# A two-network attention kernel: zero products while the first keys load, first loads reordered over two queues, first K^T copied from PSUM, key tails and weight conversions re-timed

## The chip, the cores and the metric

The kernel runs on one core of a Trainium2 chip. The metric is the device time of one execution in microseconds (us). The kernel before took 880.57 us (median of three runs, 880.42 to 881.54).

A core has five engines that run their own instruction streams and meet at semaphores: TensorE (PE, with its weight loads shown as PEld), VectorE (DVE), ScalarE (ACT), GpSimd (POOL) and SyncE (SP). SP and ACT issue the transfers here; 16 DMA engines carry them out.

## The reference

Three stages follow each other: windowed attention, a feed-forward network with g(h) = h·cos(h), and one with g(h) = relu(h)². Shapes: 4 batches, 8 heads, 512 local and 32 global positions, head size 64; the networks take 2176 tokens of 512 features through 2048 hidden ones.

```python
k_all, v_all = concat([k_g, k_l]), concat([v_g, v_l])
out_g = softmax(scale * q_g @ k_all.T) @ v_all
s_ll = where(|pos_i - pos_j| <= 32, scale * q_l @ k_l.T, -1e9)
out_l = softmax(concat([scale * q_l @ k_g.T, s_ll])) @ concat([v_g, v_l])
x = concat([out_g, out_l]) in token order       # 2176 x 512
h = x @ moe_w_in;  x = (h * cos(h)) @ moe_w_out
h = maximum(x @ moe2_w_in, 0);  out = (h * h) @ moe2_w_out
```

## The kernel before, in words

**Attention.** Heads are worked in pairs p = 0 to 15 (`divmod(p, 4)` gives batch and pair). Four heads of one batch, two pairs, are a group; there are eight. A group's keys and queries arrive in natural layout (`kn`, `qn`, two buffers each), are transposed on PE (`tr_k` L295, `tr_q` L338), and leave PSUM as `kT` and `qT`. `kT` holds, for each of eight blocks of 64 positions, three pieces: the block (`k_evac`, ACT, L306), the next block (`k_copy`, POOL, L321) and the 32 global keys (POOL, L323). The piece after the last block is the "tail" of K: its own small load (`load_ktn`, L367), a transpose (`ttail`, L350) and a copy into `kT` by POOL (L331). The values come in twice: `va` from DRAM (`load_v`, L270 and L273) and `vb`, the same rows moved by 64 partitions, by a copy inside the chip (`copy_v`, L280 and L281) that needs `va` complete. `vgz` (L286) has the global values.

**Steps.** The list of items is per group Local, Local, Local, Local, Global: 40 in all. A loop over steps s issues, for each step, parts of several items at fixed distances (`CFG["lag"]`) and in a fixed order (`CFG["order"]`): item s gets its scores S (L388, for a Global L514) and its softmax, item s-2 its transposes (`tw`, L456), item s-3 their copies out of PSUM (ACT, L462 and L466), item s-4 its output products (`o`, L472 with `vgz`, L484 with `va`, then with `vb`; a Global's `og`, L590). Since each engine runs its instructions in this order, one that waits holds up all behind it.

**Loads.** SP has nearly all loads in one queue, in the order of the program; ACT issues only the first group's queries. Before the loop stand the loads of group 0 (in two halves of two heads), its tail and values, and the keys of group 1; in the loop's first steps `vgz`, the queries of group 1 and the copies `vb` follow.

**Weights of the first network.** They arrive as pairs of 32-bit words and are converted during attention in six pieces: `conv_load` (L117, L122), `conv_u` (POOL, L142), `conv_s` (ACT, L147), then DVE and POOL steps. `piece` asks for the load at step 5 + 3i and for the first conversions two steps after it; `put` finds for each the first step from there that has room on its engine. `thalves` splits tokens for the first network and asks for their store to DRAM (`x_store`, L720) in the step after the last part is made.

**Networks.** From about 160 us on PE is the full engine (L823 and L915), and a planner lays out the instructions. The last block has 640 tokens in five tiles of 128; each tile's sum is made by DVE (L926) and stored by SP at once (L1004). The tile with the global rows is stored in four pieces (L1008).

Of the kernel before, what the change touches and what calls it, by code (L numbers as in the profile page):

```python
# [11 lines left out]
F32 = mybir.dt.float32  # L12
# [3 lines left out]
AF = mybir.ActivationFunctionType  # L16
# [4 lines left out]
P = 128  # L21
# [31 lines left out]
def kernel(  # L53
# [14 lines left out]
    nc = tc.nc  # L68
    B, H, SL, D = q_l.shape
    SG = q_g.shape[2]  # L70
# [167 lines left out]
    kn, qn, kT, qT, tks = {}, {}, {}, {}, {}  # L238


    def load_k(gi, sub=4):
        b, h0 = gi // 2, 4 * (gi % 2)
        t = fp.tile([P, 4, 4, D], F32, tag="kn", name="kn", bufs=2)
        kn[gi] = t
        for i in range(0, 4, sub):
            d, g = slice(i, i + sub), slice(h0 + i, h0 + i + sub)
            nc.sync.dma_start(t[0:SG, 0, d], k_g[b, g].rearrange("h p d -> p h d"))
            for c in range(4):
                r0 = SG if c == 0 else 0
                nc.sync.dma_start(  # L250
                    t[r0:P, c, d],
                    k_l[b, g, P * c - SG + r0 : P * c + P - SG].rearrange("h p d -> p h d"),
                )

    def load_q(gi, queue=nc.sync, heads=((0, 4),)):
        b, h0 = gi // 2, 4 * (gi % 2)
        if gi not in qn:
            qn[gi] = fp.tile([P, 4, 4, D], F32, tag="qn", name="qn", bufs=2)
        u = qn[gi]
        for i, sub in heads:  # L260
            d, g = slice(i, i + sub), slice(h0 + i, h0 + i + sub)
            for c in range(4):
                queue.dma_start(
                    u[:, c, d], q_l[b, g, P * c : P * c + P].rearrange("h p d -> p h d")
                )

    def load_v(gi):
        b, h0 = gi // 2, 4 * (gi % 2)
# [22 lines left out]
    def tr_k(p):  # L291
# [9 lines left out]
        kT[p] = t  # L301
        tks[p] = tk

    def k_evac(p):
        t, tk = kT[p], tks.pop(p)
        nc.scalar.activation(  # L306
            t[:, :, 0:64], tk.rearrange("p (j q) -> p j q", q=64), AF.Copy
        )
        if CFG["kb"] == "A":
            nc.scalar.activation(  # L310
                t[:, :, 128:KTB], tk[:, 0:SG].unsqueeze(1).to_broadcast([P, 8, SG]), AF.Copy
            )
        elif CFG["kb"] == "D":
            nc.vector.tensor_copy(
                t[:, :, 128:KTB], tk[:, 0:SG].unsqueeze(1).to_broadcast([P, 8, SG])
            )

    def k_copy(p):
        t = kT[p]
        one = dict(scalar1=1.0, scalar2=1.0, op0=ALU.mult, op1=ALU.mult)  # L320
        nc.gpsimd.tensor_scalar(t[:, 0:7, 64:128], t[:, 1:8, 0:64], **one)  # L321
        if CFG["kb"] == "P":
            nc.gpsimd.tensor_scalar(  # L323
                t[:, :, 128:KTB], t[:, 0, 0:SG].unsqueeze(1).to_broadcast([P, 8, SG]), **one
            )
        if p > 1:
            k_tail(p)
# [275 lines left out]
            )  # L603


    load_q(0, nc.scalar, ((0, 2),))
    load_k(0, 2)
    nc.vector.memset(halfpi, 0.5 * math.pi)
    nc.scalar.activation(warm, halfpi, AF.Exp)
    load_q(0, nc.scalar, ((2, 2),))  # L610
    load_ktn(0)
    load_qgn(0)
    load_v(0)
    load_k(1)
    make_identity(nc, ident)
    nc.gpsimd.memset(masks[0], 0.0)
    for h in range(2):
        s = slice(64 * h, 64 * h + 64)
# [9 lines left out]
        nc.vector.tensor_copy(masks[i], masks[0])  # L628
    nc.vector.memset(masks[1][0:64, 0:32], NEG)
    nc.vector.memset(masks[2][64:128, 96:128], NEG)  # L630
    nc.vector.memset(qgbd, 0.0)

    nc.gpsimd.memset(ktail, 0.0)
    nc.gpsimd.memset(VGZ[0], 0.0)
    nc.vector.memset(VGZ[1], 0.0)
    for t in VA:
        nc.vector.memset(t[32:64, 4], 0.0)

    items = []
    due_tr, due_load = {}, {}  # L640
# [155 lines left out]
    class Step:  # L796
# [99 lines left out]
        def jobs(self):  # L896

            if self.net == 0:
                return [(e, t) for t in (1, 0) for e in range(NK)]
            tiles = range(2 * self.n // P)  # L900
            late = [j for j in tiles if j * P >= self.n]
            return [(j, 1) for j in late] + [(j, 0) for j in tiles if j not in late]

        def job(self, j, t, k):
            n = self.n
# [11 lines left out]
        def y_out(self, j, t, eng):  # L917
            n, c0 = self.n, self.c0
            y = self.r.pop(("y", j, t))
            if self.net == 0:  # L920
                y, dst = y[:, 0:n], xt[:, j, c0 + t * n : c0 + t * n + n]
            else:
                y = y.rearrange("p (k t) -> p k t", k=NK)
                dst = xt[:, :, c0 + j * P : c0 + j * P + P]
            if not self.first():
                V.tensor_tensor(dst, y, dst, op=ALU.add)  # L926
            elif eng == "A":
                A.activation(dst, y, AF.Copy)
            else:
                V.tensor_copy(dst, y)  # L930
            if self.net == 1 and self.q == NQ - 1:
                store(c0 // P + j, dst)

        def first(self):
            return self.K % (NG // 2) == 0 and self.q % 2 == 0
# [61 lines left out]

    free_s = {}

    def store(t, y):  # L1000
        if t * P < NLOC:
            b, j = divmod(t * P, SL)
            r0 = b * (SL + SG) + SG + j
            nc.sync.dma_start(out[r0 : r0 + P, :].rearrange("p (k t) -> p k t", k=NK), y)  # L1004
        else:
            for b in range(B):
                r0 = b * (SL + SG)
                nc.sync.dma_start(  # L1008
                    out[r0 : r0 + SG, :].rearrange("p (k t) -> p k t", k=NK),
                    y[SG * b : SG * b + SG],  # L1010
                )
# [263 lines left out]
    def piece(i, *needs):  # L1275
        k = ATT[i]
        s = max(5 + 3 * i, read.get(i - 2, 0) + 1)
        bg["BG"].setdefault(s, []).append(lambda: conv_load(*k))
        u = put("BG", {"G": 0.64}, lambda e: conv_u(*k, "G"), s + 2, *needs)
        c = put("BG", {"A": 0.66}, lambda e: conv_s(*k), max(s + 2, summed.get(i - 2, 0) + 1))  # L1280
        v = put("CB", {"V": 0.41}, lambda e: conv_v(*k), u, c - 1)
        o = read[i] = put("CB", {"V": 0.68}, lambda e: conv_o(*k), u, c - 1, v - 1)
        summed[i] = put("CC", {"G": 1.28}, lambda e: conv_c(*k), s + 2, v, o)
        return summed[i]
# [21 lines left out]
    def thalves(m, first, *needs):  # L1306
        h = put("CB", {"A": 0.81}, lambda e: x_hi(0, m), first, *needs)
        los = [put("CB", VG(384), lambda e, kk=kk: x_lo(0, m, kk, e), 0, h) for kk in range(2)]
        bg["CB"].setdefault(max(los) + 1, []).append(lambda: x_store(0, m))
        return max(los)  # L1310

    def tsums(m, first, *needs):
# [23 lines left out]
    for s in range(L["TRK"], NI + L["OE"]):  # L1336
        due = lambda k: due_tr.get(s - k)
        qe = []
        for c in CFG["order"]:
# [3 lines left out]
            elif c in ("TRK", "TRQ", "KEV", "KC", "QE"):  # L1343
                p = due(L[c])
                if p is None:
                    continue
                if c == "TRK":
                    tr_k(p)
                elif c == "TRQ":
                    qe = tr_q(p)  # L1350
                elif c == "KEV":
                    k_evac(p)
                elif c == "KC":
# [8 lines left out]
            else:  # L1362
# [18 lines left out]
                        op()  # L1381
                else:
                    dict(NM=i.norm, TM=i.t_mm, TE=i.t_evac, OM=i.o_mm, OE=i.o_evac)[c]()
        if s == -3:
            load_vg(0)
        if s == -2:
            load_q(1)
        if s == -1:
            copy_v(0)
        if s in (4, 14, 24):  # L1390
            load_ktn(s // 10 + 1)
        if s in (7, 17, 27):
            load_qgn(s // 10 + 1)
# [54 lines left out]
```

## Time and profile before

| | us |
|---|---|
| median of three runs | 880.57 |
| the profiled execution | 878.93 |
| its span, first to last instruction | 876.9 |
| PE busy | 851.4 (97%) |
| DVE, POOL, ACT busy | 655.9, 584.1, 531.3 |

The busy shares are averages over the whole run. Attention fills roughly the first 145 us; there no engine is full throughout. In the networks PE is busy without a break. The time between the profiled execution's own figure and its span, 2.0 us, lies outside the instructions.

### The profile page before, as it was taken

The page shows a single profiled execution, that of the slowest core. Times are in us where ns is not written, and L with a number is a line of the kernel's source. Part 1 is how long each engine was busy: PE and PEld are TensorE (multiplying, and loading weights), DVE is VectorE, ACT ScalarE, POOL GpSimd, SP SyncE. Part 2 cuts the span into 40 slices and gives each one's busy share as a digit, 9 for nine tenths or more (in the row PEclk, how much of TensorE's full clock was granted, in tenths as well). Part 3 has the DMA queues.
Part 4 walks back from the last instruction along what each step waited for, and adds up shares of the span by engine and source line. Part 5 has one row for each costly group of instructions (what it writes and reads, how often), then busy time and mean ns, then how long its engine had stood idle before and what let it go on. Part 6 is the DMA issues. An engine that isn't in the chain of part 4 may idle for free.

```text
span 876.9 us, 17093 instructions
## 1 busy us (share of the span) xinstructions
PE 851.4 (97%) x6008; PEld 782.2 (89%) x6008; DVE 655.9 (75%) x1410; ACT 531.3 (61%) x1274; POOL 584.1 (67%) x665
## 2 busy tenths in 40 slices
PE   7899999999999999999999999999999999999997
PEld 4677777899999999999999998889888989898886
DVE  6678998899788687967778798986755767454544
ACT  5678887887777566656655767655544554443331
POOL 5578899799977663758358899986545647431221
PEclk9999999999999999999999999999999999999999
DMA  7988564457865776568627457567863687447732
GB/s 166 203 203 196 143 191 159 157 215 258 298 234 183 240 293 231 186 198 300 249 100 259 197 173 278 181 208 257 285 205 128 253 298 220 127 170 245 226 116 73
DMA packets 134309, 181.99 MB, mean 208 GB/s; under 512 B 61008, under 2 KB 114768, under 8 KB 134224
## 3 DMA queue, kind: packets, MB, share of 16 engines
q1 hardware_dynamic: 132048, 180.38, 62.9%
q8 instruction: 47, 0.77, 0.4%
q10 hardware_dynamic: 2176, 0.52, 0.3%
q14 instruction: 38, 0.31, 0.1%
HBM read 141.03 MB, written 35.65 MB: 201 GB/s over the span
## 4 chain that ended last, share of the span: by engine, by line
PE 81%; DVE 8%; POOL 5%; ACT 2%; DMA 1%; issue 1%; SPq 1%; ACTq 0%; POOLq 0%; DVEq 0%
PE y L915 40%; PE hb L823 15%; PE he L823 10%; PE ha L823 10%; DVE pt L404 2%; PE s L388 1%; POOL g L172 1%; POOL xs L172 1%; DVE st L428 1%; POOL wf L163 1%; PE o L472 1%; PE o L484 1%; DMA vb<-va 1%; PE og L590 1%; PE tw L456 1%
## 5 line engine op out<-in xcount | busy, mean ns | idle before, releaser
L172 POOL TENSOR_TENSOR g<-cr,g 128x384 fp32r<-128x384 f32 (+1 forms) x192 | 204.2, 1076 | 144.8 <-ACT g L874 139.2
L926 DVE TENSOR_TENSOR xt<-y,xt 128x384 f32<-128x384 f32 (+2 forms) x287 | 170.6, 596 | 97.3 <-PE y L915 95.4
L915 PE MATMUL y<-g,wo 128*128 128x384 f32 (+1 forms) x1152 | 219.1, 327 | 0.3 <-DVE wo L172 0.3
L915 PE MATMUL y<-wo,g 128*128 128x512 f32 x816 | 209.4, 393 | 0.0
L915 PEld LDWEIGHTS y<-g,wo 128*128 128x128 f32 x1152 | 194.1, 188 | 1.3 <-DVE wo L172 0.5
L915 PEld LDWEIGHTS y<-wo,g 128*128 128x128 f32 x816 | 150.0, 188 | 24.1
L823 PE MATMUL hb<-xs,wi 128*128 128x384 f32 (+1 forms) x864 | 166.4, 327 | 1.4 <-ACT cr L863 1.2
L823 PEld LDWEIGHTS hb<-xs,wi 128*128 128x128 f32 x864 | 146.8, 188 | 7.6 <-ACT cr L863 1.6
L823 PE MATMUL he<-xs,wi 128*128 128x384 f32 (+1 forms) x576 | 111.0, 327 | 1.7 <-DVE cr L866 0.9
L823 PE MATMUL ha<-xs,wi 128*128 128x384 f32 (+1 forms) x576 | 110.9, 327 | 1.2 <-DVE cr L866 0.7
L874 ACT ACTIVATE g<-cr 128x384 fp32r<-128x384 f32 (+1 forms) x192 | 93.8, 501 | 19.4 <-DVE cr L866 18.2
L823 PEld LDWEIGHTS he<-xs,wi 128*128 128x128 f32 x576 | 98.0, 188 | 6.2 <-DVE cr L866 1.5
L163 POOL TENSOR_TENSOR wf<-wf,cc 128x512 uint32<-128x512 uint32 x64 | 88.2, 1383 | 22.7 <-DVE wf L151 17.0
L823 PEld LDWEIGHTS ha<-xs,wi 128*128 128x128 f32 x576 | 97.6, 188 | 4.0 <-DVE cr L866 1.0
L860 ACT ACTIVATE cr<-cr,halfpi 128x384 f32<-128x384 f32 (+1 forms) x96 | 55.9, 593 | 11.2 <-DVE cr L855 10.0
L156 DVE SCALAR_TENSOR_TENSOR cc<-raw,cc 128x512 uint32<-128x512 uint32 x64 | 61.5, 966 | 0.1
L414 ACT ACTIVATE pt<-pt,st 128x160 f32<-128x160 f32 x128 | 53.1, 421 | 7.0 <-DVE st L404 6.9
L147 ACT ACTIVATE cc<-raw 128x512 uint32<-128x512 uint32 x64 | 42.4, 670 | 19.0 <-DMA raw<-in_moe_w_in_dram 9.7
L151 DVE TENSOR_SCALAR wf<-wf 128x512 uint32<-128x512 uint32 x64 | 49.4, 775 | 5.2 <-POOL wf L142 4.2
L831 ACT ACTIVATE s<-hb 128x384 f32<-128x384 f32 (+1 forms) x48 | 22.7, 473 | 48.1 <-PE hb L823 48.0
L831 ACT ACTIVATE s<-he 128x384 f32<-128x384 f32 (+1 forms) x48 | 22.6, 472 | 32.5 <-PE he L823 32.3
L172 POOL TENSOR_TENSOR wo<-wf,wo 128x512 fp32r<-128x512 f32 x14 | 19.4, 1388 | 33.9 <-ACT wo L205 33.8
(142 smaller groups left out, 1348.0 us busy)
## 6 DMA issues: line engine op xcount, KB each, us to landing
xs<-xs_T SPq DMA_DIRECT2D x48, 768.0 KB, 6.2
xs<-xs_B SPq DMA_DIRECT2D x36, 768.0 KB, 6.0
raw<-in_moe_w_in_dram SPq DMA_DIRECT2D x32, 512.0 KB, 5.2
raw<-in_moe_w_out_dram SPq DMA_DIRECT2D x32, 512.0 KB, 4.9
xs<-xs_T SPq DMA_DIRECT2D x24, 640.0 KB, 5.7
xs_T<-xs SPq DMA_DIRECT2D x16, 768.0 KB, 3.9
xs<-xs_B SPq DMA_DIRECT2D x18, 640.0 KB, 5.8
xs_B<-xs SPq DMA_DIRECT2D x12, 768.0 KB, 4.2
```

Of the source, the lines that this page charges most:

```text
L147: A.activation(v, raw[q, m, c][:, :, 0].bitcast(U32), AF.Copy, scale=2.0**-29)
L151: V.tensor_scalar(u, u, 3, None, op0=ALU.logical_shift_left)
L156: V.scalar_tensor_tensor(v, t[:, :, 1].bitcast(U32), 0x80000000, v, op0=ALU.bitwise_and, op1=ALU.bitwise_or,)
L163: G.tensor_tensor(u, u, v, op=ALU.add)
L172: eng.tensor_tensor(lo, x, hi.bitcast(F32), op=ALU.subtract)
L414: nc.scalar.activation(self.pt[:, u, :], self.pt[:, u, :], AF.Exp, bias=self.st[:, 0, u : u + 1], scale=-1.0, accum_out=self.st[:, 1, u : ...
L823: nc.tensor.matmul(out, lhsT=w[:, ws, c : c + P], rhs=xs[:, xh, kk, 0:n], start=start and k == 0, stop=k == 5, skip_group_check=True,)
L831: A.activation(self.sb[name], self.hold(bank_name), AF.Copy)
L860: A.activation(self.r[key], self.r[key], AF.Sin, bias=halfpi, scale=TWOPI)
L874: A.activation(GT[s, f][0][:, th * n : th * n + n], self.r[key], AF.Copy)
L915: nc.tensor.matmul(o, lhsT=l, rhs=r, start=k == 0, stop=k == 5)
L926: V.tensor_tensor(dst, y, dst, op=ALU.add)
```

## The change

Five edits. (1) PE gets products of a zeroed tile with itself into an unused PSUM bank: six ahead of the first transposes of K, two after them, two after the first transposes of Q. (2) The loads ahead of the loop are reordered and cut differently: while two heads are loaded, one transfer takes all whole 128-row chunks of one head instead of one chunk of two heads; the first K and Q are shared by SP and ACT; the queries of group 1 and the copies `vb` come ahead of the second half of group 1's keys and queries; memsets move from DVE to POOL and change places. (3) For p = 0 the second and third piece of `kT` are copied from PSUM by DVE and ACT instead of from `kT` by POOL. (4) The tail load comes three steps sooner, the conversions of a weight piece stand three steps after its load instead of two, and no store of split tokens is asked for before step 33. (5) In the last step the two late tiles change places, and the stores of odd tiles go through ACT's queue.

```diff
+    def whole(dst, src, c0, queues):
+        n = dst.shape[2]
+        if n == 2:
+            for h, queue in enumerate(queues):
+                queue.dma_start(dst[:, c0:4, h], src[h].rearrange("(c p) d -> p c d", p=P))
+        else:
+            for c in range(c0, 4):
+                r = P * (c - c0)
+                queues[0].dma_start(dst[:, c], src[:, r : r + P].rearrange("h p d -> p h d"))
+
+    def load_k(gi, h=0, n=4, queues=(nc.sync, nc.sync)):
...
+        nc.sync.dma_start(t[0:SG, 0], k_g[b, g].rearrange("h p d -> p h d"))
+        nc.sync.dma_start(t[SG:P, 0], k_l[b, g, 0 : P - SG].rearrange("h p d -> p h d"))
+        whole(t, k_l[b, g, P - SG : SL - SG], 1, queues)
...
     def k_evac(p):
...
+        if p == 0:
+            nc.vector.tensor_copy(t[:, 0:7, 64:128], tk4(tk)[:, 1:8])
+            nc.scalar.activation(
+                t[:, :, 128:KTB],
+                tk[:, 0:SG].unsqueeze(1).to_broadcast([P, 8, SG]),
+                AF.Copy,
+            )
     def k_copy(p):
+        if p == 0:
+            return
...
-    load_q(0, nc.scalar, ((0, 2),))
-    load_k(0, 2)
+    load_k(0, 0, 2, (nc.scalar, nc.scalar))
+    load_q(0, 0, 2, (nc.sync, nc.scalar))
+    idle = cpool.tile([P, P], F32, name="idle")
+    nc.vector.memset(idle, 0.0)
     nc.vector.memset(halfpi, 0.5 * math.pi)
     nc.scalar.activation(warm, halfpi, AF.Exp)
-    load_q(0, nc.scalar, ((2, 2),))
+    load_k(0, 2, 2)
+    load_q(0, 2, 2, (nc.scalar, nc.scalar))
+    make_identity(nc, ident)
+    for t in VA:
+        nc.gpsimd.memset(t[32:64, 4], 0.0)
+    nc.gpsimd.memset(VGZ[0], 0.0)
     load_ktn(0)
     load_qgn(0)
     load_v(0)
-    load_k(1)
-    make_identity(nc, ident)
+    load_k(1, 0, 2)
+    load_q(1, 0, 2)
+    load_vg(0)
+    copy_v(0)
+    load_k(1, 2, 2)
+    load_q(1, 2, 2)
+    nc.vector.memset(qgbd, 0.0)
...
+    def spin(n):
+        t = ps.tile([P, 512], F32, tag=f"bank{BO[1]}", name="spin")[:, 0:P]
+        for _ in range(n):
+            nc.tensor.matmul(t, lhsT=idle, rhs=idle, start=True, stop=True)
...
-            return [(j, 1) for j in late] + [(j, 0) for j in tiles if j not in late]
+            return [(j, 1) for j in late[::-1]] + [(j, 0) for j in tiles if j not in late]
...
-                store(c0 // P + j, dst)
+                last = self.s == NS - 1 and j % 2
+                store(c0 // P + j, dst, nc.scalar if last else nc.sync)
...
-        u = put("BG", {"G": 0.64}, lambda e: conv_u(*k, "G"), s + 2, *needs)
-        c = put("BG", {"A": 0.66}, lambda e: conv_s(*k), max(s + 2, summed.get(i - 2, 0) + 1))
+        u = put("BG", {"G": 0.64}, lambda e: conv_u(*k, "G"), s + 3, *needs)
+        c = put("BG", {"A": 0.66}, lambda e: conv_s(*k), max(s + 3, summed.get(i - 2, 0) + 1))
...
-        bg["CB"].setdefault(max(los) + 1, []).append(lambda: x_store(0, m))
+        bg["CB"].setdefault(max(33, max(los) + 1), []).append(lambda: x_store(0, m))
...
+                    if p == 0:
+                        spin(6)
                     tr_k(p)
+                    if p == 0:
+                        spin(2)
...
-        if s == -3:
-            load_vg(0)
-        if s == -2:
-            load_q(1)
-        if s == -1:
-            copy_v(0)
-        if s in (4, 14, 24):
+        if s in (1, 11, 21):
             load_ktn(s // 10 + 1)
```

SP's queue after the values of group 0 (`kn`, `qn` of group 1 first, then of group 2; `va_93`, `vb_95` are group 0's). Before:

```order
L247 DMA kn<-in_k_g_dram 32x4x64
L250 DMA kn<-in_k_l_dram 96x4x64
L250 DMA kn<-in_k_l_dram 128x4x64 x3
L286 DMA vgz_97<-in_v_g_dram 32x4x64 x4
L263 DMA qn<-in_q_l_dram 128x4x64 x4
L280 DMA vb_95<-va_93 64x1024
L281 DMA vb_95<-va_93 64x1024
```

And after the change:

```order
L257 DMA kn<-in_k_g_dram 32x2x64
L258 DMA kn<-in_k_l_dram 96x2x64
L246 DMA kn<-in_k_l_dram 128x3x64 x2
L246 DMA qn<-in_q_l_dram 128x4x64 x2
L286 DMA vgz_97<-in_v_g_dram 32x4x64 x4
L280 DMA vb_95<-va_93 64x1024
L281 DMA vb_95<-va_93 64x1024
L257 DMA kn<-in_k_g_dram 32x2x64
L258 DMA kn<-in_k_l_dram 96x2x64
L246 DMA kn<-in_k_l_dram 128x3x64 x2
L246 DMA qn<-in_q_l_dram 128x4x64 x2
```

The copies `vb` moved ahead of half of group 1's keys and queries.

PE at its start (`tk`, `tq`: transposes of K and Q; `s`: scores; `spin`: the zero products). Before:

```order
L295 MATMUL tk<-ident,kn 128x128 x4
L338 MATMUL tq<-ident,qn 128x128 x4
L295 MATMUL tk<-ident,kn 128x128 x4
L388 MATMUL s<-kT,qT 64x160 x8
L350 MATMUL ttail<-ident,ktn 128x32 x4
```

And after the change:

```order
L663 MATMUL spin<-idle 128x128 x6
L295 MATMUL tk<-ident,kn 128x128 x4
L663 MATMUL spin<-idle 128x128 x2
L350 MATMUL tq<-ident,qn 128x128 x4
L663 MATMUL spin<-idle 128x128 x2
L295 MATMUL tk<-ident,kn 128x128 x4
L400 MATMUL s<-kT,qT 64x160 x8
```

The zero products were put in; the rest of PE's order is the same to the end.

ACT around the conversion `cc` of the third weight piece (steps 13 and 14; `tws`, `tgs` copies of an item's transposes, `kT` the copy of the next keys). Before:

```order
L462 ACTIVATE tws<-tw 128x512
L466 ACTIVATE tgs<-tg 128x128
L147 ACTIVATE cc<-raw 128x512
L414 ACTIVATE pt,st<-pt,st 128x160 x4
L462 ACTIVATE tws<-tw 128x512
L466 ACTIVATE tgs<-tg 128x128
L306 ACTIVATE kT<-tk 128x8x64
```

And after the change:

```order
L474 ACTIVATE tws<-tw 128x512
L478 ACTIVATE tgs<-tg 128x128
L426 ACTIVATE pt,st<-pt,st 128x160 x4
L474 ACTIVATE tws<-tw 128x512
L478 ACTIVATE tgs<-tg 128x128
L147 ACTIVATE cc<-raw 128x512
L308 ACTIVATE kT<-tk 128x8x64
```

The conversion moved behind one step's exponentials and copies.

## Rows read from the trace of the kernel before

**Rows 1.** Stretches: busy us of PE, PEld, DVE, ACT, POOL; clock, DMA share, GB/s.

```profile
20.00:40.00 20.00, 16.39 (x258) 13.04 (x258) 12.79 (x64) 13.51 (x55) 10.84 (x27) 1.00 0.90 198
80.00:100.00 20.00, 17.50 (x280) 14.00 (x277) 18.04 (x74) 15.98 (x58) 15.73 (x29) 1.00 0.66 135
600.00:800.00 200.00, 200.00 (x1027) 179.93 (x1026) 125.11 (x203) 95.01 (x197) 103.61 (x97) 1.00 0.65 215
```

**Rows 2.** The same view of the start.

```profile
0.00:2.00 2.00, 0.00 (x0) 0.00 (x0) 0.06 (x1) 0.00 (x0) 1.30 (x9) 1.00 0.06 13
0.00:10.00 10.00, 5.41 (x28) 2.93 (x28) 5.29 (x10) 2.68 (x4) 4.97 (x16) 1.00 0.61 136
14.00:16.00 2.00, 2.00 (x18) 1.56 (x19) 1.52 (x12) 1.26 (x7) 1.35 (x4) 1.00 0.57 124
```

**Rows 3.** Chain of waits, then timeline (start, us, instruction, idle before): first outputs.

```profile
17.73 5.27 DMA vb<-va
...
23.04 0.34 PE L484 MATMUL o<-tws,vb 128*64 128x64 f32 x4 [1.34 <-DMA vb<-va]
```

**Rows 4.** Timeline: PE's transposes of K early and later.

```profile
15.13 1.11 PE L295 MATMUL tk<-ident,kn 128*128 128x128 f32 x4
...
35.14 0.66 PE L295 MATMUL tk<-ident,kn 128*128 128x128 f32 x4
```

**Rows 5.** Timeline and transfers: second tail (issue, KB and us to landing, reader).

```profile
27.39 0.44 SPq L367 DMA_DIRECT2D ktn<-in_k_l_dram  x1
...
ktn<-in_k_l_dram SPq DMA_DIRECT2D x1, 64.0 KB, 3.8
...
31.31 0.40 PE L350 MATMUL ttail<-ident,ktn 32*128 32x32 f32 x4 [1.98 <-DVE pt L443]
```

**Rows 6.** Timeline and transfers: second copy of group 1's values, and its reader.

```profile
32.60 0.54 SPq L281 DMA_DIRECT2D vb<-va  x1
...
vb<-va SPq DMA_DIRECT2D x1, 256.0 KB, 5.8
...
41.11 0.29 PE L484 MATMUL o<-tws,vb 128*64 128x64 f32 x4
```

**Rows 7.** Timeline around the third weight piece, then the stretch behind it.

```profile
52.73 0.37 SPq L122 DMA_DIRECT2D raw<-in_moe_w_out_dram  x1
...
57.39 0.67 ACT L147 ACTIVATE cc<-raw 128x512 uint32<-128x512 uint32 x1 [3.10 <-DMA raw<-in_moe_w_out_dram]
...
59.48 0.66 PE L295 MATMUL tk<-ident,kn 128*128 128x128 f32 x4 [1.70 <-DVE qT L344]
...
60.25 0.58 ACT L306 ACTIVATE kT<-tk 128x512 f32<-128x512 f32 x1
...
60.00:64.00 4.00, 3.90 (x41) 2.85 (x41) 3.37 (x17) 3.74 (x14) 3.33 (x7) 0.65 0.84 224
```

**Rows 8.** Timeline: token stores, last values, their reader; the page's DMA line.

```profile
117.08 0.54 SPq L281 DMA_DIRECT2D vb<-va  x1
123.73 0.34 SPq L720 DMA_DIRECT2D xs_T<-xs  x1
...
131.24 0.55 SPq L281 DMA_DIRECT2D vb<-va  x1
...
143.41 0.39 PE L472 MATMUL o<-tgs,vgz 128*64 128x128 f32 x4
...
DMA packets 134309, 181.99 MB, mean 208 GB/s; under 512 B 61008, under 2 KB 114768, under 8 KB 134224
```

**Rows 9.** The end: stores, last sum, one stretch.

```profile
868.26 2.60 SPq L1008 DMA_DIRECT2D out_dram<-xt  x4
870.95 1.95 SPq L1004 DMA_DIRECT2D out_dram<-xt  x3
871.62 0.69 DVE L926 TENSOR_TENSOR xt<-y,xt 128x512 f32<-128x512 f32 x1 [0.67 <-PE y L915]
...
873.00:874.00 1.00, 0.00 (x0) 0.00 (x0) 0.00 (x0) 0.00 (x0) 0.00 (x0) 0.80 1.03 287
```

More of the change, by code (lines that the diff above doesn't have):

```diff
@@ L238, with load_q @@
     kn, qn, kT, qT, tks = {}, {}, {}, {}, {}
[L241 to L256, printed above, removed]
+    def whole(dst, src, c0, queues):
[8 more added lines that the diff above has]
+    def load_k(gi, h=0, n=4, queues=(nc.sync, nc.sync)):
+        b, g = gi // 2, slice(4 * (gi % 2) + h, 4 * (gi % 2) + h + n)
+        if gi not in kn:
+            kn[gi] = fp.tile([P, 4, 4, D], F32, tag="kn", name="kn", bufs=2)
+        t = kn[gi][:, :, h : h + n]
+        nc.sync.dma_start(t[0:SG, 0], k_g[b, g].rearrange("h p d -> p h d"))
+        nc.sync.dma_start(t[SG:P, 0], k_l[b, g, 0 : P - SG].rearrange("h p d -> p h d"))
+        whole(t, k_l[b, g, P - SG : SL - SG], 1, queues)
+    def load_q(gi, h=0, n=4, queues=(nc.sync, nc.sync)):
+        b, g = gi // 2, slice(4 * (gi % 2) + h, 4 * (gi % 2) + h + n)
         if gi not in qn:
             qn[gi] = fp.tile([P, 4, 4, D], F32, tag="qn", name="qn", bufs=2)
[L259 to L265, printed above, removed]
+        whole(qn[gi][:, :, h : h + n], q_l[b, g], 0, queues)
     def load_v(gi):
@@ L302, in tr_k @@
         tks[p] = tk
+    tk4 = lambda tk: tk.rearrange("p (j q) -> p j q", q=64)
     def k_evac(p):
@@ L306, in k_evac @@
         nc.scalar.activation(
-            t[:, :, 0:64], tk.rearrange("p (j q) -> p j q", q=64), AF.Copy
+            t[:, :, 0:64], tk4(tk), AF.Copy
         )
+        if p == 0:
[5 more added lines that the diff above has]
+            )
         if CFG["kb"] == "A":
@@ L630 @@
     nc.vector.memset(masks[2][64:128, 96:128], NEG)
-    nc.vector.memset(qgbd, 0.0)
     nc.gpsimd.memset(ktail, 0.0)
[L634 to L637, printed above, removed]
+    nc.gpsimd.memset(VGZ[1], 0.0)
+    def spin(n):
+        t = ps.tile([P, 512], F32, tag=f"bank{BO[1]}", name="spin")[:, 0:P]
+        for _ in range(n):
+            nc.tensor.matmul(t, lhsT=idle, rhs=idle, start=True, stop=True)
     items = []
@@ L998, with store @@
     free_s = {}
-    def store(t, y):
+    def store(t, y, queue=nc.sync):
         if t * P < NLOC:
@@ L1003, in store @@
             r0 = b * (SL + SG) + SG + j
-            nc.sync.dma_start(out[r0 : r0 + P, :].rearrange("p (k t) -> p k t", k=NK), y)
+            queue.dma_start(out[r0 : r0 + P, :].rearrange("p (k t) -> p k t", k=NK), y)
         else:
@@ L1347 @@
                 if c == "TRK":
+                    if p == 0:
+                        spin(6)
                     tr_k(p)
+                    if p == 0:
+                        spin(2)
                 elif c == "TRQ":
                     qe = tr_q(p)
+                    if p == 0:
+                        spin(2)
                 elif c == "KEV":
```

## Prediction, made before the changed kernel ran

> **What bounds the kernel now.** I first read the busy time by stretches. In the networks PE is the limit: busy 200.00 of 200.00 us from 600 to 800 [rows 1]. PE's order there is the same before and after, so nothing the change does to the networks counts but the last stores; what it wins ahead of them is carried to the end. From 60 us to the end of attention DVE is the fullest, 18.04 of 20 us, and the DMA engines are 0.66 busy [rows 1]. That stretch keeps its work, moved by at most a step. From 20 to 40 us it is the other way round: DMA 0.90 busy at 198 GB/s while PE has 16.39 of 20, DVE 12.79 and POOL 10.84 [rows 1]. So the start is bounded by the stream of loads, and there I read who waits for a landing. Four places show it. The first output products wait 1.34 us at 23.04 for `vb`, issued at 17.73 and 5.27 us under way [rows 3]. The second tail's transposes wait 1.98 us: their load is issued at 27.39 and lands 3.8 us later, at 31.2; the view names a DVE product as the releaser, but the transposes start at 31.31, right behind the landing [rows 5]. The second copy of group 1's values lands at 32.60 + 5.8 = 38.4 and is read at 41.11, 2.7 us later [rows 6]. ACT waits 3.10 us for the third weight piece, until 57.39; PE, behind it, stands still 1.70 us and then runs four microseconds at a mean granted clock of 0.65 [rows 7], partly at the lower of its two levels (1.2 and 2.4 GHz).
>
> **How I measure the stream.** Let D be how much earlier the same bytes have landed. Nothing moves before 2 us (13 GB/s), yet by 10 us the mean is 136 GB/s, 1.36 MB [rows 2]. At the 198 GB/s of the full stretch, eight microseconds carry 1.58 MB; the difference of 0.22 MB is worth 1.1 us. From 14 to 16 us the rate is 124 GB/s, where SP issues four small `vgz` loads [rows 2]; that is 0.15 MB or 0.7 us more, which a fuller queue ahead may fill. I take D = 2.0, rounded up for transfers that are fewer and larger at the very start. Bounds: -0.5, if transfers cut by heads move no faster and the two queues hinder each other, and 3.5, if the later gaps (0.90 busy is not 1.00) close too.
>
> **The change part by part.** *Order of the loads.* Up to the second `vb` the queues carried K and Q of group 0 (0.52 MB each), tail and global queries 0.13, `va` 0.56, K of group 1 0.52, `vgz` 0.13, Q of group 1 0.52, `vb` 0.52: 3.4 MB. Half of group 1's K and Q, 0.52 MB, goes behind; at 198 GB/s that is 2.6 us. `vb` lands at 23.00 - 2.6 - 2.0 = 18.4. The products would have run at 23.04 - 1.34 = 21.7 without the wait. They hang on the transposes of group 1's first keys, ahead of which only half of its keys is loaded now (0.26 MB less, 1.3 us), with some 1.2 us of D by then: 2.5 us sooner, so 19.2, a gain of 3.8 (bounds 1.3, the wait alone, and 4.6, the landing at 18.4). What is moved back, half of K and Q, stands right behind `vb`, 0.52 MB ahead of no one who is earlier than about 20 us.
>
> *Tail.* Its load now stands ahead of `va` of group 1 (0.56 MB, 2.8 us). It lands at 31.2 - 2.8 - 2.0 = 26.4; the transposes would want it at 31.31 - 1.98 - 3.8 = 25.5. A wait of 0.9 us stays; the gain so far is 31.31 - 26.5 = 4.8 us.
>
> *Group 1's second value copy.* Its bytes ahead are the same, so it lands at 38.4 - 2.0 = 36.4, against a reader at 41.11 - 4.8 = 36.3: no more than 0.1 us lost.
>
> *Third weight piece.* The load stands where it stood: 57.3 - 2.0 = 55.3. Its conversion stands one step later, behind four exponentials and two copies. Before, those ran from the end of the conversion at 58.0 to the key copy at 60.25 [rows 7], 2.2 us; run during the wait they would be over at 57.39 - 3.10 + 2.2 = 56.5, and, 4.8 us sooner, at 51.7. So ACT still waits, 3.6 us, but with less behind it: conversion from 55.3 to 56.0, then the key copy, which stood at 60.25. The gain is 4.3 us. This wait decides: it takes 0.5 us of what was won and would hide a start that wins only 1.3 us. The clock afterwards: the wait may again let PE go down; bounds 0 and 1.4 (4 us at 0.65 instead of 1.00), I take 0.5, as PE's stand is as likely to stay as not.
>
> *Zero products.* No row has this form. The nearest are K's transposes: four in 1.11 us early and 0.66 later [rows 4], 0.17 to 0.28 us each; a product of four times the passes would be 0.66 to 1.1. I take 0.4, near the double of the early row. Six run before any key has landed and cost nothing; four stand between transposes, 1.6 us on PE (0.7 to 4.4), at worst all of the start's gain but the `vb` order. If they raise the clock they give it back: each four transposes save 0.45. I set their net at zero, and the wait for the third piece covers either sign up to 3.6 us.
>
> *First K^T from PSUM, memsets.* DVE's new copy stands behind the two mask copies, which wait for POOL's masks, now behind three memsets. All are over before the second keys' transposes, which gate the first scores either way; at nothing, and 1 us if that cover is gone (less than the 3.6).
>
> *Stores of split tokens after step 33.* Four transfers of 768 KB now stand ahead of the last values. SP was free from 117.6 to 123.73 [rows 8], so three of them flow in that gap; the last copy, issued at 131.24, is read at 143.41, 12.2 us later. At nothing; the price without that cover is a rival below.
>
> *The end.* Four small stores hold SP from 868.26 for 2.60 us, and the sums follow each other at 0.67 + 0.69 = 1.36 us, the last ending at 872.31; so the store due at 869.59 is issued at 870.95, and three drain together at 287 GB/s [rows 9], 0.9 us each. With the odd tiles on ACT and the small stores first, the last store follows an empty queue: 0.5 us (bounds 0 and 1.4).
>
> **Sum.** 4.3 + 0.5 + 0.5 = 5.3 us. The profiled execution took 878.93, 1.64 below the median of 880.57; 873.6 on its scale, and by the median **875.3 us**.
>
> **Rivals.** *A: the stream is no faster (D = 0).* Then the third piece lands at 57.3, the key copy follows at 58.0 instead of 60.25, 2.2 us, with 0.5 for the end 2.7: 877.9. For it: 0.90 busy in the full stretch [rows 1]; against it: 0.61 busy in the first 10 us [rows 2]. The Trainium skill (DMA: Bandwidth & Descriptors, section "Issuing engines are not separate DMA queues") says that transfers started from several engines run on the same 16 DMA engines, and that a second issuer saves only the time of issuing. By that rule taken alone the second queue gives this rival's time; the rows agree from 20 us on and leave room before 10 us, where the engines were idle for lack of issues.
>
> *B: the stream wins more (D = 3.5).* The third piece lands at 53.8, the key copy at 54.5: 5.8, with 0.8 for the clock and 0.5 for the end 7.1: 873.5. For it: small transfers are the slow ones, and there are fewer; against it: the bytes are the same and pieces of 256 bytes stay.
>
> *C: the last values come late.* If the four stores all begin at 123.73, because SP reaches them only when the last part is made, 3.15 MB at the page's mean of 208 GB/s [rows 8] take 15.1 us. `va` behind them, `vb` behind `va`: landing at 131.24 + 5.3 + 15.1 = 151.6 against a reader at 143.41, a stall of 8.2: 875.3 + 8.2 = 883.5, slower. It decides once the values lose more than about 7 us to the stores (12.2 to the reader, less the copy's own 5.3); against it stands the free stretch of SP.
>
> *D: nothing arrives.* The DVE-bound steps absorb what came early, for instance because weight work, a step later, crowds the last ones: 880.1, the end's 0.5 alone. Against it: that stretch has the same work and begins earlier.
>
> **Chances.** Forecast 0.47, A 0.22, B 0.19, C 0.05, D 0.07. About 0.2% (1.8 us) is what a measurement can tell from no change. Faster takes the forecast, B, and nine tenths of A: 0.86. The same takes D and the rest of A: 0.09. Slower is C: 0.05. The range reaches past B by the bound of the clock and past A to the edge of no change: 871.5 to 878.9.
>
> **What would show it.** Right: the first product with `vb` near 19 us; the tail's transposes near 26.5; the conversion of the third piece still waiting on ACT, ending near 55.3; a mean of some 165 GB/s or more in the first 10 us; the last store ending 3.6 us instead of 4.6 after the last sum. Wrong: no DMA wait left before 60 us (B), or the third piece landing at 57 (A); a wait of PE for `vb` near 140 (C). A gain at 60 us that is gone at 150 would mean that the steps between, not the start, set the time.

## The result, and the profile after

The changed kernel takes 873.25 us (median of 4 runs, 873.11 to 873.39) against 880.89 for the kernel before, run beside it (4 runs, 880.42 to 881.54): ratio 0.9913, 95% interval 0.9896 to 0.993, some 7.6 us. The profiled executions differ by less, 878.93 and 873.37, 5.6 us: in the runs beside the experiments the kernel before lay between 877.06 and 881.98, and its profile is one of the shorter ones. Its medians there were 879.28 to 879.93, so the gain is rather 6.0 to 6.7 us. The forecast was 875.3, and 873.6 on the profile's scale. The time is near, but its main terms are wrong: most of the gain comes from an edit that the sum gave no line of its own, and the start, on which the sum was built, brings next to nothing.

First the start. Stretches of the changed kernel, with the columns of [rows 1], then two of the kernel before:

```profile
0.00:10.00 10.00, 7.92 (x64) 6.65 (x66) 5.60 (x18) 3.76 (x9) 6.32 (x20) 1.00 0.86 171
10.00:20.00 10.00, 7.53 (x103) 5.41 (x95) 7.77 (x43) 8.05 (x35) 5.75 (x17) 1.00 0.69 153
20.00:30.00 10.00, 6.87 (x94) 5.49 (x95) 4.71 (x27) 5.03 (x19) 4.78 (x12) 0.93 0.83 186
20.00:40.00 20.00, 16.87 (x245) 13.55 (x246) 11.05 (x56) 12.83 (x50) 9.56 (x24) 0.91 0.87 193
80.00:100.00 20.00, 19.14 (x312) 15.12 (x314) 18.57 (x80) 17.84 (x65) 18.84 (x33) 1.00 0.70 147
```

```profile
10.00:20.00 10.00, 8.88 (x82) 6.86 (x78) 6.69 (x42) 7.31 (x32) 5.07 (x15) 1.00 0.86 193
20.00:30.00 10.00, 7.70 (x109) 5.71 (x107) 5.95 (x30) 5.59 (x23) 4.79 (x12) 1.00 0.92 204
```

The first ten microseconds moved 1.71 MB instead of 1.36 [rows 2], as hoped. The next ten gave it all back: 1.53 MB against 1.93, so that at 20 us both had moved the same, 3.24 and 3.29 MB, and by 30 us the changed kernel is behind by 0.23 MB. The last two rows of the first fence answer to [rows 1]: from 20 to 40 us little is different, and from 80 to 100 us PE, ACT and POOL are busier by 1.6 to 3.1 us. That second stretch is where most of the gain is made.

The landings at which the prediction stopped, in the changed kernel's timeline (start, us, instruction, idle before it): first product with `vb`, second tail, third weight piece, key copy, and the scores behind it.

```profile
19.16 0.29 PE L496 MATMUL o<-tws,vb 128*64 128x64 f32 x4
...
28.42 0.47 PE L362 MATMUL ttail<-ident,ktn 32*128 32x32 f32 x4 [2.25 <-DMA ktn<-in_k_l_dram]
...
59.12 0.66 ACT L147 ACTIVATE cc<-raw 128x512 uint32<-128x512 uint32 x1 [3.93 <-DMA raw<-in_moe_w_out_dram]
59.69 0.58 ACT L308 ACTIVATE kT<-tk 128x512 f32<-128x512 f32 x1
...
60.82 0.77 PE L400 MATMUL s<-kT,qT 64*64 64x160 f32 x14 [2.90 <-ACT ptg L551]
```

The first product starts at 19.16, where 19.2 was forecast, 3.9 us ahead of [rows 3]. The tail comes at 28.42 instead of 26.5, and the third piece at 59.12 instead of 55.3: later than before, when its conversion started at 57.39 [rows 7]. Yet the key copy, now behind that conversion with nothing between, is 0.6 us ahead of its old place.

Then the place that the prediction passed over. The kernel before around 82 us, by POOL, DVE, PE and ACT:

```profile
79.86 1.28 POOL L172 TENSOR_TENSOR wi<-ws,wi 128x512 fp32r<-128x512 f32 x1
81.11 0.56 POOL L321 TENSOR_SCALAR kT<-kT 128x448 f32<-128x448 f32 x1
81.64 0.40 POOL L323 TENSOR_SCALAR kT<-kT 128x256 f32<-128x256 f32 x1
82.01 0.24 POOL L331 TENSOR_SCALAR kT<-ktail 128x64 f32<-128x64 f32 x1
82.22 0.69 POOL L142 TENSOR_SCALAR wf<-raw 128x512 f32<-128x512 f32 x1
...
82.94 0.95 DVE L151 TENSOR_SCALAR wf<-wf 128x512 uint32<-128x512 uint32 x1 [1.40 <-POOL wf L142]
...
84.14 0.67 DVE L344 COPY qT<-tq 128x512 f32<-128x512 f32 x1
...
84.96 0.63 PE L571 MATMUL twg<-ident,ptg 128*128 128x128 f32 x4 [1.41 <-DVE qT L344]
...
85.15 0.43 ACT L414 ACTIVATE pt<-pt,st 128x160 f32<-128x160 f32 x1 [2.10 <-DVE st L404]
...
86.25 0.40 POOL L436 TENSOR_TENSOR pg<-pt,st 128x128 f32<-128x128 f32 x1 [2.65 <-DVE st L431]
```

POOL splits a weight (1.28 us) and makes three key copies before it can unpack the fifth weight piece (L142). DVE, in order, stands 1.40 us before the instruction that reads the unpacked words, and behind it stand the query copy and the maxima; PE loses 1.41 us, ACT 2.10, POOL itself 2.65. In the changed kernel the unpacking and its reader come one step later:

```profile
81.15 1.27 POOL L172 TENSOR_TENSOR wi<-ws,wi 128x512 fp32r<-128x512 f32 x1
...
81.90 0.66 PE L583 MATMUL twg<-ident,ptg 128*128 128x128 f32 x4
...
82.40 0.68 POOL L142 TENSOR_SCALAR wf<-raw 128x512 f32<-128x512 f32 x1
...
83.11 0.61 DVE L151 TENSOR_SCALAR wf<-wf 128x512 uint32<-128x512 uint32 x1
```

`twg` no longer waits and starts 3.06 us sooner, before the unpacking instead of behind it, and the reader on DVE has no wait. The sixth piece has one instead, where the kernel before had none (its reader starts at 94.23 there):

```profile
93.59 0.62 DVE L151 TENSOR_SCALAR wf<-wf 128x512 uint32<-128x512 uint32 x1 [0.90 <-POOL wf L142]
```

Last the end, as in [rows 9], stores by queue and the last sum:

```profile
862.55 2.60 SPq L1036 DMA_DIRECT2D out_dram<-xt  x4
...
863.91 3.26 ACTq L1032 DMA_DIRECT2D out_dram<-xt  x2
...
865.27 3.28 SPq L1032 DMA_DIRECT2D out_dram<-xt  x2
...
867.27 0.69 DVE L953 TENSOR_TENSOR xt<-y,xt 128x512 f32<-128x512 f32 x1 [0.67 <-PE y L942]
```

The last sum ends at 867.96 and the span at 871.55, 3.6 us later; before it was 872.31 and 876.89, 4.6 us.

### The profile page after: what moved, and what is told of

The parts are those of the page before. It is cut to its first block, busy times and chain, and to the rows that moved or that the text cites. A ratio compares the mean times of both kernels' runs of the same rounds, so it can differ in the third digit from the quotient of the medians.

```text
span 871.5 us, 17134 instructions
## 1 busy us (share of the span) xinstructions
PE 849.9 (98%) x6028; PEld 783.9 (90%) x6028; DVE 656.7 (75%) x1409; ACT 531.5 (61%) x1275; POOL 583.5 (67%) x666
## 4 chain that ended last, share of the span: by engine, by line
PE 82%; DVE 6%; POOL 4%; ACT 2%; DMA 2%; issue 1%; SPq 1%; POOLq 0%; ACTq 0%
PE y L942 41%; PE hb L850 16%; PE ha L850 10%; PE he L850 10%; DVE pt L416 1%; POOL xs L172 1%; ACT pt L426 1%; PE s L400 1%; PE o L484 1%; POOL g L172 1%; DMA kn<-in_k_l_dram 1%; PE o L496 1%; POOL xr L724 1%; PE og L602 1%; POOL wf L163 1%
## 5 line engine op out<-in xcount | busy, mean ns | idle before, releaser
L156 DVE SCALAR_TENSOR_TENSOR cc<-raw,cc 128x512 uint32<-128x512 uint32 x64 | 61.9, 973 | 0.0
L172 POOL TENSOR_TENSOR wi<-ws,wi 128x512 fp32r<-128x512 f32 x23 | 30.8, 1342 | 15.9 <-ACT wi L196 12.3
```

The source lines that it names most:

```text
L156: V.scalar_tensor_tensor(v, t[:, :, 1].bitcast(U32), 0x80000000, v, op0=ALU.bitwise_and, op1=ALU.bitwise_or,)
L172: eng.tensor_tensor(lo, x, hi.bitcast(F32), op=ALU.subtract)
```

## The experiments

The lead of each profiled kernel over the profile of before (us; minus is behind), read at the starts of five output sums on DVE and at the end of the last sum of all. The column heads are their times in the kernel before; below, each run is named by what it changes. Each run's time was measured beside the kernel before, not beside the changed kernel.

| kernel | 23.9 | 42.6 | 61.9 | 78.9 | 91.4 | last sum | time, median |
|---|---|---|---|---|---|---|---|
| changed | 3.5 | 0.9 | 1.5 | 0.8 | 5.1 | 4.35 | 873.25 |
| e1 changed, conversions early | 3.2 | 1.7 | -1.2 | -1.2 | -1.3 | -1.1 | 879.67 |
| e2 before, conversions late | 0.4 | -1.3 | 1.4 | 0.9 | 5.2 | 4.3 | 874.49 |
| e3 changed, tail sooner | 3.7 | 2.1 | 2.1 | 1.3 | 5.7 | 4.9 | 873.42 |
| e4 changed, no zero products | -0.5 | 1.4 | 1.6 | -0.2 | 4.1 | 3.3 | 873.88 |
| e5 changed, third piece sooner | 3.7 | 0.7 | 3.3 | 2.6 | 6.9 | 7.0 | 871.20 |
| e6 as e1, one unpacking later | 3.2 | 0.6 | -2.3 | -2.1 | 1.5 | 0.0 | 876.83 |
| e7 changed, end and stores as before | 3.8 | -0.6 | 0.5 | -1.2 | 3.1 | 2.8 | 874.51 |
| e8 changed, `vgz` issued by ACT | -1.4 | 1.1 | 2.0 | 1.2 | 5.5 | 5.5 | 872.23 |
| e9 e3 and e5 together | 3.6 | 1.4 | 2.7 | 2.2 | 6.5 | 5.7 | 871.62 |
| e10 before, conversions late, third piece sooner | 0.4 | 0.7 | 3.8 | 2.7 | 7.1 | 7.1 | 872.40 |
| e12 before, one unpacking later | 0.5 | 1.0 | 0.9 | 1.6 | 4.9 | 2.15 | 876.89 |
| e13 e9, first piece later | 3.1 | -2.9 | -1.7 | -2.8 | -0.3 | -3.7 | 880.91 |

Two executions of one program differ too. Up to 78.9 us the kernel before and e12 have the same instructions, so have e1 and e6, and so have the changed kernel and e7; yet their leads there are 1.6, 0.9 and 2.0 us apart. Differences of that size between two rows of a column show nothing by themselves. The column at 91.4 is a peak for the runs that gain there: at 115 us the lead of the changed kernel is 4.3 and that of e12 3.7.

**The conversions put back.** In `piece`, for POOL's unpacking and ACT's conversion:

```
-        u = put(... conv_u ..., s + 3, *needs)
-        c = put(... conv_s ..., max(s + 3, ...))
+        u = put(... conv_u ..., s + 2, *needs)
+        c = put(... conv_s ..., max(s + 2, ...))
```

> The changed kernel with the weight conversions back at two steps after their load instead of three; all else as changed. Theory 1 (the gain between 78 and 92 us, where the lead over the kernel before grew from 0.8 to 5.1 us, comes from the conversions' new step, which takes the 1.40 us wait of DVE for POOL's unpacking at 82.94 away): the wait comes back, the lead at the output sums near 85 to 140 us stays near 1 to 2 us instead of 4.4, and the time is 875.5 to 877. Theory 2 (the lead comes from the earlier start and the shorter stream of loads; the steps merely show it later): 872.5 to 874, with the lead near 4 us at 100. Either way ACT waits for the third weight piece about as long as before (3 to 4 us near 57).

879.67 us (877.36 to 882.16), ratio to before 1.0002 [0.9985, 1.002]: all of the gain is gone, more than theory 1 had, though the new end is still in. At 24 us the lead is 3.2 us, as in the changed kernel; at 62 us the run is 1.2 us behind, and it stays there. The wait at POOL's unpacking is back to the hundredth:

```profile
84.19 0.95 DVE L151 TENSOR_SCALAR wf<-wf 128x512 uint32<-128x512 uint32 x1 [1.40 <-POOL wf L142]
```

**The conversions alone.** The same two lines of the kernel before, from `s + 2` to `s + 3`, and nothing else.

> The kernel before with one edit alone: the weight conversions three steps after their load instead of two. Theory 1: the 1.40 us wait of DVE near 82 goes, twg no longer waits 1.41 us at 84.96, and the time falls by 2.5 to 3.5 us, to about 877.5 against about 880.8. Theory 2: the time stays within 1 us of before, since nothing arrives sooner.

874.49 us (873.74 to 875.62), ratio 0.9936 [0.9914, 0.9957]: 5.3 us less than the kernel before beside it (879.76), almost twice what theory 1 expected. It starts 0.4 us ahead of before where the changed kernel has 3.5, and from 62 us on the two run within 0.3 us of each other. The end's 1.0 us is most of what is left between the two times. With e1 this settles where the gain comes from.

**The second tail sooner.**

```
     copy_v(0)
+    load_ktn(1)
     load_k(1, 2, 2)
...
-        if s in (1, 11, 21):
+        if s in (11, 21):
```

> The changed kernel with the second tail's load ahead of the second half of group 1's keys in the prologue. It should land near 20 us, so the 2.25 us wait of PE at 28.42 goes, and with it, if the wait is what lowers the clock, the stretch at the lower level from 28.6 to 32.0. Theory 1 (what binds next is the third weight piece, landing at 59.04, and ACT's wait of 3.93 us for it): ACT's wait grows to 5 to 6 us, and the time stays within 0.8 us of 873.25. Theory 2 (the start's lead is carried to the end): 870.5 to 871.8.

873.42 us (872.78 to 874.71), as theory 1 had it, but by another wait than it named: ACT's wait for the third piece fell to 2.3 us, and what took the tail's 2.25 us was the second copy of group 1's values.

```profile
39.75 0.34 PE L496 MATMUL o<-tws,vb 128*64 128x64 f32 x4 [3.23 <-DMA vb<-va]
```

**Without the zero products.** The three calls of `spin` left out.

> The changed kernel without the ten products of zeros. The changed kernel's clock is at the upper level from 4.71 us, the one before it from 16.86. Theory 1: without the products the clock rises late again, K's first transposes take 1.1 us a group instead of 0.66 and the first scores come about 1 us later, but the waits for the second tail (2.25 us) and the third weight piece (3.93 us) absorb it: 872.7 to 873.8. Theory 2 (they bring part of the gain): 874.2 to 875.5. Theory 3 (they cost PE time between the transposes, 0.3 us each): 872 to 872.7.

873.88 us (872.66 to 874.54), ranges that overlap: not told apart. The granted clock is at the upper level from 23.07 us instead of 4.71, and at 24 us 4.0 us of lead are missing; at 42.6 us none is (1.4 against 0.9). The 1 us that is missing later comes behind another stretch at the lower level from 60.6 to 64.0.

**The third weight piece sooner.**

```
-        bg["BG"].setdefault(s, []).append(lambda: conv_load(*k))
+        bg["BG"].setdefault(s - (i == 2), []).append(lambda: conv_load(*k))
```

> The changed kernel with the third weight piece's load issued one step sooner: ahead of group 3's keys, group 2's second value copy and group 3's queries (1.5 MB) instead of behind them; its conversion stays where it is. In all four runs in which ACT waited for this piece, the lead or lag at 60 us followed its landing to 0.1 us (landings 57.31 before, 59.04 changed, 58.56 and 58.52 in the two runs beside). Theory 1 (this landing is the funnel at which the early lead is lost): it lands near 48 to 50, ACT's 3.9 us wait goes, the lead at 62 us grows from 1.4 to about 3.5 us and is kept, 870.8 to 871.8. Theory 2 (the whole stream is late, not this piece; keys, values or queries, now 0.5 MB later, take the wait over): lead at 62 us still 1 to 2 us, 872.7 to 874.

871.20 us (870.73 to 871.9), ratio to before 0.9907 [0.9892, 0.9922], and 2.05 below the changed kernel (the ranges do not overlap; the two ratios, 0.9907 and 0.9913, which have the scatter of the kernel before in them, do): theory 1, by the lead of 3.3 us at 62 us. Another 0.4 us comes at 155 us, where the changed kernel's clock fell to the lower level for 3.4 us and here it did not. The piece lands at 51.0 and the conversion no longer waits; the next wait is 0.59 us of PE, for values that are now 2.9 us later:

```profile
55.29 0.69 ACT L147 ACTIVATE cc<-raw 128x512 uint32<-128x512 uint32 x1
...
56.63 0.34 PE L496 MATMUL o<-tws,vb 128*64 128x64 f32 x4 [0.59 <-DMA vb<-va]
```

**One unpacking.** As e1, but for the fifth piece:

```
-        u = put(... conv_u ..., s + 2, *needs)
+        u = put(... conv_u ..., 21 if i == 4 else s + 2, *needs)
```

> The changed kernel with the conversions back at two steps after their load (as in the run that gave 879.7), except that the fifth piece's unpacking on POOL is put at step 21 instead of 20, and what hangs on it follows. At step 20 POOL also has the global row's product (L575, 0.75 us). Theory 1 (the 3.5 us between 78 and 92 us are lost at this one place: POOL's queue at step 20 makes DVE wait 1.40 us, behind which the query copy, twg and the softmax stand): the place is clean, 876 to 877, with the lag of 1.1 us over the kernel before at 70 us turning into a lead of about 2.4 at 92. Theory 2 (the later step pays over the whole attention, a little at each piece): 878.5 to 880.

876.83 us (875.78 to 878.89): theory 1, 2.8 us from one piece's step by the medians. The lag of 2.1 at 79 us is a lead of 1.5 at 91; in this profile it is 0.0 at the last sum, 1.1 better than e1. POOL now does the global row's product first, and the unpacking, at 85.01, has until DVE comes to it:

```profile
84.32 0.72 POOL L575 TENSOR_SCALAR ptg<-ptg,stg 128x544 f32<-128x544 f32 x1
85.01 0.68 POOL L142 TENSOR_SCALAR wf<-raw 128x512 f32<-128x512 f32 x1
...
86.43 0.62 DVE L151 TENSOR_SCALAR wf<-wf 128x512 uint32<-128x512 uint32 x1
```

**End and token stores undone** (old order of the late tiles, `last = False`, and no `max(33, ...)`).

> The changed kernel with the last step's jobs and stores as before (old order of the late tiles, all stores on SP) and with the split tokens' stores as soon as they are made. From the traces, the last store ends 4.6 us after the last sum before and 3.5 in the changed kernel: undone, 4.6 again, 1.05 us more, 874.0 to 874.5, and nothing from the token stores (the lead between 106 and 140 us unchanged to 0.3). Rival: the token stores bring something of their own (they no longer stand ahead of values on SP): 875 or more, lead at 140 us smaller.

874.51 us (873.99 to 875.79), 1.26 more. The span ends 4.5 us after the last sum, against 3.6: the end's part is 0.9. This execution was also 1.5 to 2 us later from 42 us on, after PE's clock had stood at the lower level from 28.3 to 35.1, twice as long as in the changed kernel; that is ahead of any token store. The token stores show nothing of their own: from 79 us to 141 the lead grows by 4.6, in the changed kernel by 4.4.

**Global values by ACT** (`load_vg(0, nc.scalar)`).

> The changed kernel with the four loads of global values (32 KB each) of the prologue issued by ACT instead of SP. In the changed kernel SP issues one transfer about every 0.5 us from 9 to 22 us, and the DMA engines are only 0.6 to 0.8 busy there; in 20 us it has moved 3.24 MB, the kernel before 3.28, although it was 0.35 MB ahead at 10 us. Theory 1 (the stream's lead is lost to the issuing of more and smaller transfers by one queue): second value copy and tail land about 1.5 to 2 us sooner, tail near 26.5 instead of 28.29, while the first scores come up to 2 us later because ACT issues ahead of its first copy. Theory 2 (the engines set the pace): the tail lands within 0.5 us of 28.3. The time under both: 872.5 to 874, since the third weight piece sets 60 us.

872.23 us (872.03 to 873.7), and the tail lands at 28.08, as theory 2 had it. It doesn't settle the cause. SP has four issues fewer here, but ahead of them it waited longer for earlier landings (2.7 us in all, against 0.9), so its first load of group 1's keys goes out at 10.20 instead of 8.95, and it comes to the tail at 24.54, as in the changed kernel (24.49). From 10 to 20 us the rate rose as theory 1 wants, from 153 to 183 GB/s, and then fell below.

```profile
10.00:20.00 10.00, 7.85 (x81) 5.11 (x85) 6.11 (x33) 6.83 (x27) 3.56 (x10) 0.83 0.77 183
20.00:30.00 10.00, 9.37 (x135) 7.25 (x127) 7.08 (x36) 7.54 (x31) 6.64 (x18) 1.00 0.75 165
```

What it does show is plainer: 4.9 us lost at the start cost nothing at 42 us.

**Tail and third piece together** (both edits).

> The changed kernel with both moves: the second tail's keys ahead of group 1's second half, and the third weight piece's load one step sooner (871.2 alone). Theory 1 (each landing in its turn takes the lead: with the tail early, the second copy of group 1's values, landing near 39.6, makes PE wait 3.2 us, as in the run with the tail alone): lead at 45 us as in the run with the third piece alone, time within 0.8 of 871.2. Theory 2 (the tail's 2.4 us wait and the low clock behind it still cost, now that the third piece no longer covers them): 869 to 870.2.

871.62 us (869.99 to 872.05): theory 1. PE waits 3.37 us for the second value copy, and the 3.5 us won ahead of it are gone at 46 us.

**Only two edits in the kernel before**: conversions at `s + 3` and the third piece a step sooner.

> The kernel before with two edits: conversions three steps after their load, and the third weight piece's load one step sooner. No new start, no new end. It tells what the new start is worth once the third piece is out of the way. Theory 1 (the start's lead is then carried to the end: 2.2 us at 57 us): the run of before with the conversions alone did not wait for that piece, so nothing is gained here, 873.8 to 875, and the 871.2 of the other holds 2.2 us of the start and 1.0 of the end. Theory 2 (the start is worth nothing even then): 871.8 to 872.8, the end's 1.0 being all that differs.

872.40 us (871.58 to 872.84), ratio 0.9921 [0.9905, 0.9938]: theory 2, and theory 1 wrong. Against e5 it is 3.3 us behind at 20 us, level with it at 34.8, and 0.1 ahead at the last sum; the 1.2 us between the two times are, but for 0.2, the end's 1.0. The edit also gained 2.1 us over e2, which had not waited for that piece; most of it shows at 42 us, ahead of the moved load, where e2's clock had been at the lower level from 32.3 to 35.7. How much of the 2.1 is the edit's stays open.

**One unpacking in the kernel before** (the line of e6).

> The kernel before with one instruction's step changed: the fifth piece's unpacking on POOL at step 21 instead of 20, and what hangs on it. Theory 1 (POOL's queue at step 20 costs 2.8 us, as the changed kernel with the same edit showed: 879.67 to 876.83): 876.5 to 877.7, the lead appearing between 80 and 92 us and none at 62. Theory 2 (that run's gain had another cause): 879 to 881.

876.89 us (876.11 to 878.47), ratio 0.9979 [0.9967, 0.9991]: theory 1, 2.4 us from one instruction's place by the medians, 1.8 by the ratio. The lead grows by 3.3 between 79 and 91 us, by 2.1 to 115; a part goes again in the first network (4.1 at 146 us, 2.3 at 295), which I didn't follow.

**The first weight piece later** (e9, with piece 0 loaded at step 6 instead of 5 and converted one step later).

> The run with tail and third piece moved (871.6), with the first weight piece's load (512 KB) moved behind group 1's second value copy and group 2's queries, and its conversion one step later. It asks whether the early start can be cashed when nothing that is wanted late stands ahead of what is wanted early. Theory 1 (the 3.4 us wait for the second value copy at 39.75 is the place where the lead of 3.5 us, gained by the early tail, goes): the copy lands 2.5 us sooner, near 37, the wait falls to about 1 us, lead at 45 us 2 us better, time 869 to 870.2. Theory 2 (the next landing, the first or second weight piece, takes it): 870.8 to 872.5, with ACT or POOL waiting for a weight piece between 38 and 50.

880.91 us (880.25 to 882.59): outside both. The value copy's wait fell to 1.86 us, but the weight piece landed at 44.27, and ACT, POOL and through them DVE and PE stood before it:

```profile
44.29 0.66 ACT L147 ACTIVATE cc<-raw 128x512 uint32<-128x512 uint32 x1 [7.72 <-DMA raw<-in_moe_w_in_dram]
...
44.35 0.65 POOL L142 TENSOR_SCALAR wf<-raw 128x512 f32<-128x512 f32 x1 [8.49 <-DMA raw<-in_moe_w_in_dram]
...
46.00 0.81 PE L400 MATMUL s<-kT,qT 64*64 64x160 f32 x8 [4.97 <-ACT ptg L551]
```

## Why the prediction came out as it did

- **First products, 19.2: right.** Measured 19.16.
- **D = 2.0, kept from the start to the third piece: the step that failed.** By bytes D was 1.8 us at 10 us (0.35 MB at 198 GB/s) and nothing at 20; the third piece landed 1.7 us later than before, beyond the bound of -0.5. I had taken D from the empty engines of the first 10 us and let it stand, without asking what sets the pace of the queue. In the kernel before, the chain of waits that ends at the first outputs runs from one issue of SP to the next, from 5.22 to 17.73 us, about 0.5 us each:

```profile
16.52 0.51 SPq L263
17.03 0.04 issue
17.07 0.56 SPq L280
```

So the issues ahead of a landing count, not only the bytes. Ahead of the second copy `vb` SP has 32 issues before and 26 after the change, and it goes out 3.2 us sooner (17.73, now 14.57). Ahead of the queries of group 2 it has 38 in both kernels: three were spared on group 0, and K of group 1 now takes eight transfers of 16 to 96 KB instead of five. The lead is gone there (issues before and after):

```profile
22.00 2.15 SPq L263 DMA_DIRECT2D qn<-in_q_l_dram  x4
...
22.34 2.11 SPq L250 DMA_DIRECT2D qn<-in_q_l_dram  x4
```

This is read from the traces; no run tests it alone, and e8, which was meant to, doesn't. The Trainium skill (DMA: Bandwidth & Descriptors, section "Issuing engines are not separate DMA queues") says that a second issuer saves only the time of issuing. The traces agree from 20 us on: what ACT's queue gave by 10 us was gone.
- **Tail at 26.5: wrong by 1.9**, for the same D: with D at nothing the same sum has it land at 28.4, and it landed at 28.29. PE waited 2.25 us, not 0.9, and its clock then stood at the lower level for 3.4 us:

```profile
28.00:30.00 2.00, 1.58 (x20) 1.55 (x22) 0.01 (x1) 1.07 (x4) 1.33 (x4) 0.65 0.85 193
30.00:32.00 2.00, 2.00 (x20) 1.47 (x16) 0.43 (x1) 1.55 (x9) 0.00 (x0) 0.50 0.84 226
```

- **Group 1's second value copy at 36.4: late by 2.3**, at 38.66, again for D. Its reader, at 39.71, didn't wait.
- **Third piece, gain 4.3: wrong.** The key copy came 0.6 us sooner. That this wait decides was right (e5), that the start arrives there was not. In the runs that waited for it, the lead at 62 us followed the landing: e1 against before 1.2 us later with a landing 1.25 later, e3 against the changed kernel 0.6 sooner with a landing 0.5 sooner; e4, e7 and e8 against the changed kernel, e6 against e1 and e12 against before fit to 0.1. The 1.5 us measured there are not the start's either: the conversions alone give 1.4.
- **The clock behind the third piece, 0.5: nothing that shows.** The fall of the kernel before (61.23 to 64.64 us) is gone, but the lead is 1.5 us at 61.9 and 1.4 at 69.1, and the clock fell at 28.60 and 154.90 instead, 3.4 us each.
- **"That stretch keeps its work, moved by at most a step": the term that was missing.** I looked at what the step does at the third piece and priced it at nothing elsewhere; rival D even had it as a loss. The lead grows by 4.3 us between 79 and 91 us, by 3.5 to 115; e6 and e12 show that the fifth piece's unpacking alone is worth 2.8 and 2.4 by the medians. The row was there to be read: the only wait of DVE for POOL, 1.40 us, in the stretch in which DVE is the fullest engine.
- **Zero products, first K^T, token stores: nothing, right** as far as it was measured; the first K^T had no run of its own.
- **The end, 0.5: mis-sized**, 1.0 us by the traces, 0.9 in e7. The prediction's own sign, 3.6 instead of 4.6 us after the last sum, was right and contradicted its term.

So 5.3 forecast and 5.6 measured between the profiled executions agree by accident: 4.3 from the start that did not come, and some 4 that came from the step instead. By the prediction's own sign, a third piece that lands at 57 us or later, the stream was rival A's or worse; A's 877.9 us missed for the same missing term. The rest of the 7.6 is the scatter of the kernel before, over which its profile stood low. The kernel before (10 to 14 runs at a time) and e1 (10) scatter by 3.0 to 4.9 us, those with late conversions (4, 5 or 10 runs) by 0.3 to 2.3; why is open.

## What to carry to other kernels

In this kernel a lead won at the start of the stream of loads was taken by the next landing that came no sooner; ask of each later landing whether it comes sooner by the new order, not by the old lead. Where the chain of waits runs from issue to issue, count the transfers ahead of it as well as the bytes. When instructions move by a step, look in the fullest stretch for in-order engines that wait on each other, and price the step there: one instruction's place in POOL's queue was worth more than the whole new start. Two edits in the kernel before, the conversions' step and the third piece's load, give 872.4; with the rest of the change, 871.2, the fastest version measured here.

## What the hardware showed that was not expected

SP's issuing seems to stop while a block of instructions is fetched. Over 1.3 us of the changed kernel the list of DMA queues has one packet of kind "instruction" (kind, packets, MB, share of the engines), and the issue that falls into it takes 1.4 us, not 0.5:

```profile
q8 instruction: 1, 0.02, 5.6%
```

```profile
25.53 1.92 SPq L273 DMA_DIRECT2D va<-in_v_l_dram  x2
...
45.38 1.70 SPq L258 DMA_DIRECT2D kn<-in_k_l_dram  x1
```

(The first row holds two issues, 1.39 and 0.48 us.) Such packets of 16 KB are in the trace at 14.4, 25.4, 37.1, 45.4, 52.7 and 63.0 us, 8 to 18 SP transfers apart; at each an issue takes 1.4 to 1.7 us. That the block is SP's, and that its fetch is what holds the issue up, is read from these times alone. Four such stops lie ahead of the third weight piece in the kernel before and five in the changed one, where the fifth made the last issue ahead of that piece 1.74 us long instead of 0.51. It isn't the whole reason why the piece was late: e1 has four such stops ahead of it, and there it landed 1.25 us later than before all the same.
